# Four PSUM banks as tiles of their own instead of one tile, in a fused RWKV-5 and tanh-shrink kernel

## The chip, the cores and the metric

The kernel runs on one core of one Trainium2 chip. The metric is the device time of one execution in microseconds (us). The core's engines are TensorE (PE, with its weight load PEld), VectorE (DVE), ScalarE (ACT), GpSimd (POOL) and SyncE (SP, which here only issues DMAs). Each works through its own queue in order and waits for others on semaphores.

## The reference

The first half is a linear recurrence per batch and head (B = 4, H = 8, S = 768, D = 48), the second half a two-layer map of 3072 tokens (384 to 2048 to 384), all in float32:

```
for t in range(S):
    cur = einsum('bhd,bhe->bhde', u * k[t], v[t])
    y[t] = einsum('bhd,bhde->bhe', r[t], state + cur)
    state = w * state + einsum('bhd,bhe->bhde', k[t], v[t])
x = y, heads side by side            # (B*S, H*D) = (3072, 384)
h = x @ w_in                         # (3072, 2048)
out = (h - tanh(h)) @ w_out          # (3072, 384)
```

## The kernel before, in words

**Units.** The recurrence is cut into 24 units, `unit(n)`: 64 time steps of two batches each. A unit transposes r and k on TensorE (`turn`, L721), brings them to SBUF as rT (VectorE, L725, scaled by the decay) and kT (ScalarE, L734), multiplies rT with the carried state (`from_state`) and with kT (`levels`), both at L676, copies the result under a causal mask into `at` (VectorE, L875), and multiplies that with v (`outputs`) and k with v (`to_state`). Results go to xt (L812) and to the state (L839, L884), which the unit two later needs. Units 0 to 15 use a pair of PSUM banks called `x_banks` for transposes and levels; units 16 to 23 (`two`) use `yk_ps`, where all units have their outputs.

**Dense tiles.** Twelve blocks `j` of 256 tokens each pass through eight tiles of 256 hidden columns, `hidden(j, ...)`. A tile computes h (L166), five activations on ScalarE (L175 to L183) and four VectorE steps (L190 to L196), which give g = h - tanh(h) by a series where h is small. Then g is multiplied with w_out. Blocks 0 to 5 (`FIRST` = 6) do this in four passes of two tiles each over all blocks, `o` (L204), into two PSUM banks, one for each 128 tokens; after a pass each bank is collected (`empty`: ScalarE L228 or VectorE L217) and added up in SBUF. The weights are loaded and converted meanwhile (L135 to L141).

**Seven products.** Blocks 6 to 11 multiply g with w_out by seven products of half width instead of eight: GpSimd forms sums of parts of g (L239 to L243) and earlier of w_out (L263), TensorE accumulates seven products in four banks over the tiles of a block (`products`, L254, in two parts), and `collect` (L275 to L287) combines the four banks into the two outputs, in six steps. The last two tiles of block 11 use the ordinary `o`, into `yk_ps`.

**PSUM.** `ps_a` holds `x_ps` (L559: one tile of four banks; banks 0 and 1 are `x_banks[0]`, banks 2 and 3 are `x_banks[1]`, used by unit 1 and then by the outputs of `o`; the seven products use all four as `seven.ps`) and `yk_ps` (two banks). `ps_d` holds two banks for h.

**Order.** Nothing is ordered by hand. `Plan` collects tasks with an engine, a cost and predecessors (`add`), runs them forward in a model of the five queues, and improves the due times by 1000 random changes (`order`, one random number per task in each); the resulting order is then written to the queues. The semaphore waits come from the tiles that instructions read and write, not from the plan's predecessors. Where TensorE would stand still early on, the plan writes filler matmuls of the identity (L613, L614), some of them into `x_banks[1]`.

Of the kernel before, what the change touches and what calls it, by code (L numbers as in the profile page):

```python
# [143 lines left out]
class Dense:  # L144
# [99 lines left out]

    def products(self, t, part):

        n, w, mixed = self.d.DM // 2, self.w_out_sb, self.seven.mixed[:, t.f // 2]
        g, s, ps = t.g.rearrange("p (a t) -> p a t", a=4), t.s4, self.seven.ps
        b11, b21, b22 = w[:, t.f, :n], w[:, t.f + 1, :n], w[:, t.f + 1, n:]
        for bank, half, a, b in ([(0, 0, g[:, 0], b11), (1, 1, s[:, 0], mixed[:, 2]),  # L250
                                  (0, 1, s[:, 2], mixed[:, 1]), (1, 0, g[:, 3], mixed[:, 3])] if part == 0 else
                                 [(2, 0, g[:, 2], b21), (2, 1, s[:, 1], mixed[:, 0]), (3, 0, s[:, 3], b22)]):
            first = t.first and (half == 0) != (bank == 1)
            self.nc.tensor.matmul(ps[:, bank, half * n : (half + 1) * n], a, b, start=first, stop=t.last,  # L254
                                  skip_group_check=True)

    def mix(self, f, x):

# [6 lines left out]
    def collect(self, t, x):  # L265

        n, ps, V = self.d.DM // 2, self.seven.ps, self.nc.vector
        if x == 0:
            t.e, t.u = (self.work.tile([128, self.d.DM], F32, name=name, tag="part", bufs=L * FIRST) for name in "eu")
            whole = t.fs[1] == self.d.NF  # L270
            t.os = [self.work.tile([128, self.d.DM], F32, name="o", tag="o") if whole else
                    self.work.tile([128, self.d.DM], F32, name="part", tag="part", bufs=L * FIRST) for _ in range(L)]
            if not whole:
                self.sums.update({(t.j, i): t.os[i] for i in range(L)})
            self.nc.scalar.copy(t.e[:, :n], ps[:, 0, :n])  # L275
        elif x == 1:
            V.tensor_tensor(t.e[:, n:], t.e[:, :n], ps[:, 0, n : 2 * n], ALU.subtract)
        elif x == 2:
            V.tensor_tensor(t.u[:, :n], t.e[:, n:], ps[:, 1, n : 2 * n], ALU.add)
        elif x == 3:  # L280
            flat = ps.rearrange("p b n -> p (b n)")[:, 512 : 512 + 2 * (512 + n)]
            V.tensor_tensor(t.os[1].rearrange("p (i n) -> p i n", i=2), t.u[:, None, :n].to_broadcast([128, 2, n]),
                            flat.rearrange("p (i n) -> p i n", i=2)[:, :, :n], ALU.add)
        elif x == 4:
            V.tensor_tensor(t.os[0], t.e, ps[:, 2, : 2 * n], ALU.add)
        else:
            V.tensor_tensor(t.os[0][:, n:], t.os[0][:, n:], ps[:, 3, :n], ALU.add)  # L287

    def store(self, o, n, z, queue):

# [204 lines left out]
def near(ctx, tc, r, k, v, w, u, out, shared, moe_w_in, moe_w_out):  # L495
# [60 lines left out]
    before = before.bitcast(I32)[:, None, None, :].to_broadcast([128, 2, NP, SHORT])  # L556


    quad, yk_ps = (ps_a.tile([128, n, 512], F32, name=x, tag=x) for x, n in (("x_ps", 4), ("yk_ps", 2)))  # L559
    x_banks = [quad[:, :2], quad[:, 2:]]  # L560

    def new_outs(t):
        banks = yk_ps if t.j >= FIRST else x_banks[1]
        return [banks[:, i, : d.DM] for i in range(L)]

    pools = []

# [4 lines left out]
            dense.seven.mixed = pools[0].tile([128, d.NF // 2, 4, d.DM // 2], F32, name="mixed", tag="mixed")  # L572
        return pools[0]

    dense.seven = SimpleNamespace(ps=quad, pool=later)
    dense.negative = set(range(FIRST, d.NB))
    y_ps = yk_ps[:, :, :256].rearrange("e z (p t) -> e z p t", p=NP)
    kv_ps = yk_ps[:, :, 256 : 256 + NP * D].rearrange("d z (p e) -> d z p e", p=NP)
# [101 lines left out]
    def unit(n):  # L680
# [6 lines left out]
        t = SimpleNamespace(at=ats[n % 2])  # L687
        rt, vt, kw, state = rts[n % (AHEAD + 1)], vts[n % (AHEAD + 1)], kws[n % 2], states[half]
        two = n >= L * (FIRST + 2)
        banks = yk_ps if two else x_banks[n == 1]  # L690
        sign = -1.0 if slot and j in dense.negative else 1.0
        r_ps, k_ps = (banks[:, i] for i in range(2))
        lev, own_lev = (banks[:, :, at : at + 256].rearrange("s i (p t) -> s i p t", p=NP) for at in ((256, 0) if two else (0, 256)))
        none = SimpleNamespace(**{x: None for x in "r k v turn rT kw kT rk du own diag state lev cp out xt rest add decay".split()})
        b1, b2, b3 = (units[n - i] if n >= i else none for i in (1, 2, 3))
        x = SimpleNamespace(rest=None, rk=None, du=None, own=None)
# [210 lines left out]
    def finished_seven(t, x, due, pace):  # L907

        whole, now, steps, j = t.fs[1] == d.NF, x.o, [], t.j
        for i, (e, cost) in enumerate((("ACT", .3), ("DVE", .26), ("DVE", .26), ("DVE", .47), ("DVE", .47), ("DVE", .26))):  # L910
            now = add(e, cost, lambda i=i: dense.collect(t, i), [now] + (sum((stored.get((j - 1, i), []) for i in range(L)), []) if whole and not i else []), due + 3 * pace)
            steps.append(now)
        x.empty += steps
        if whole:
            for i in (1, 0):
                stored[j, i] = [add("POOL", .6, lambda z=z, i=i: dense.store(t.os[i], L * j + i, z, G),
                                    [steps[3 if i else 5]], due + 4 * pace, data=.4) for z in range(2)]

    def hidden(j, fs, f, due, pace, seven=False):
        t = dense.tile(j, fs, f)  # L920
        none = SimpleNamespace(g=None, c1=None, c2=None, cp=None, o=None, h=None, s=None, q=None, small=None, th=None, tg=None, empty=[])
        m = len(tiles)
        b1, b2, b3, b5 = (tiles[m - i] if m >= i else none for i in (1, 2, 3, 5))
        x = SimpleNamespace(empty=[])
        tiles.append(x)
        piece = f // 4 * 4 + f // 2 % 2
        now = add("PE", 1.29, lambda: dense.h(t, 0), filled[j, "all"] + [converted[piece], b1.h, b2.s, b2.th, b2.tg, b2.g] + ([flagged] if m == 1 else []), due, steps=12)
        x.h = add("PE", 1.29, lambda: dense.h(t, 1), [now], due + 1.3, steps=12)
        last_h[j] = x.h
        if m == 0:  # L930
            plan.fills += [([], tabled, fills(idle)[1:]), ([ups], now, fills(idle))]
        x.s = add("ACT", .48, lambda: dense.act(t, "s"), [x.h, b2.c1, b2.q, b2.small, b1.s])
        x.th = add("ACT", .48, lambda: dense.act(t, "th"), [x.h, b2.g, b1.th] + ([units[m].rk, units[m].kw] if m < L else []))
        x.tg = add("ACT", .48, lambda: dense.act(t, "tg"), [x.h, b2.cp, b1.tg])
        x.q = add("ACT", .63, lambda: dense.act(t, "q"), [x.s, b2.c2, b1.q])
        x.small = add("ACT", .63, lambda: dense.act(t, "small"), [x.s, b2.cp, b1.small])
        x.g = add("DVE", .6, lambda: dense.vec(t, "g"), [x.th, x.tg, b5.o, b1.g])
        x.c1 = add("DVE", .6, lambda: dense.vec(t, "c1"), [x.s, x.tg])
        x.c2 = add("DVE", .6, lambda: dense.vec(t, "c2"), [x.q, x.c1])
        x.cp = add("DVE", .65, lambda: dense.vec(t, "cp"), [x.c2, x.small, x.g])  # L940
        if seven:
            x.sg = add("POOL", .8, lambda: dense.sums_of_g(t, 0), [x.cp, b3.o, b1.cp])
            for i in (1, 2):
                x.sg = add("POOL", .5, lambda i=i: dense.sums_of_g(t, i), [x.sg])
            done = units[L * (FIRST + 2) - 1]
            now = add("PE", 1.32, lambda: dense.products(t, 0), [x.sg, mixed[f // 4], b1.o, done.cp, done.diag, done.lev] + b1.empty, due + 2 * pace, steps=16)
            x.o = add("PE", .99, lambda: dense.products(t, 1), [now], due + 2 * pace + 1.3, steps=12)
            if t.last:
                finished_seven(t, x, due, pace)
            return  # L950
        tail = [units[-1].xt, units[-1].rest, units[-1].cp] if j >= FIRST else []
        now = add("PE", 1.3, lambda: dense.o(t, 0), [x.cp, converted[piece + 2], b1.o] + b1.empty + tail + ([units[1].cp, units[1].diag] if m == 0 else []), due + 2 * pace, steps=8)
        if m == 0:
            plan.fills.append(([units[1].cp, units[1].diag], now, fills(x_banks[1][:, 0])))
        x.o = add("PE", 1.3, lambda: dense.o(t, 1), [now], due + 2 * pace + 1.3, steps=8)
        if not t.last:
            return
        whole = fs[1] == d.NF
        for i in range(L):
            ends = SimpleNamespace()  # L960

            def run(i=i, ends=ends):
                dense.empty(t, i)
                ends.o = t.o

            x.empty.append(add("DVE" if fs[0] or j == d.NB - 1 else "ACT", .47, run, [[now, x.o][i]] + stored.get((j - 1, i), []), due + 3 * pace))
            if whole and j < d.NB - 1:

                stored[j, i] = [add("POOL", .6, lambda z=z, i=i, ends=ends: dense.store(ends.o, L * j + i, z, G),
                                    [x.empty[-1]], due + 4 * pace, data=.4) for z in range(2)]  # L970
# [340 lines left out]
```

## Time and profile before

| | us |
|---|---|
| median of 3 runs | 632.31 (631.82 to 632.37) |
| the profiled execution's own time | 631.65 |
| its span | 629.9 |
| TensorE busy in the span | 597.9 |
| VectorE busy | 452.1 |
| ScalarE busy | 402.1 |
| GpSimd busy | 175.0 |
| h, L166, 1152 matmul records of 381 ns | 281.2 |
| outputs of blocks 0 to 5, L204, 384 records of 494 ns | 142.5 |
| seven products, L254, 644 records of some 326 ns | 151.1 (59.9 + 46.2 + the two groups of 92 records, 22.5 each) |

The span runs from the first to the last event of the profiled program; the own time of that execution is the device time that the runs are compared by. Times of day in the text are microseconds from the span's start. A matmul in float32 leaves two records. A line of the timeline gives the start, the length, the engine, the line of the kernel, the operation, what it writes and reads, and in square brackets how long the engine stood idle before it and which instruction released it. Lengths of neighbouring instructions on an engine can overlap. A busy TensorE sets the time here: on the chain that ended last, it has 84% of the span.

### The profile page before, as it was taken

What the parts mean: (1) busy time and instruction counts of PE and PEld (TensorE: products, weight loads), DVE (VectorE), ACT (ScalarE), POOL (GpSimd) and SP (SyncE); (2) the same over time, 40 slices, a digit from 0 to 9 for tenths busy, and PEclk for the clock granted to TensorE, in tenths of its full rate; (3) what the DMA queues carried; (4) which work ended last, traced back from release to release, by engine and by line L of the source; (5) the groups of instructions that cost most, each with busy time, mean ns of one, the idle gap of its engine ahead of it and who ended that gap; (6) DMA issues with size and microseconds to landing.
All of it is one profiled execution on the core that took longest, in us unless ns stands there. A gap on an engine that the chain in (4) does not pass through costs nothing.

```text
span 629.9 us, 13869 instructions
## 1 busy us (share of the span) xinstructions
PE 597.9 (95%) x5489; PEld 478.1 (76%) x5489; DVE 452.1 (72%) x729; ACT 402.1 (64%) x896; POOL 175.0 (28%) x313
## 2 busy tenths in 40 slices
PE   8797889899999999999999899999999999999996
PEld 7465666577767677776766689999899899889995
DVE  5588777799798768888566675776776675656664
ACT  2396767878668557665555675586576576656751
POOL 5001211130001000029313163344354255335440
PEclk9799999999999999999999999999999999999999
DMA  6963459446003300000224320022021010000101
GB/s 125 221 109 64 90 109 218 81 92 154 0 20 96 86 0 1 2 0 1 50 55 86 65 52 14 1 55 43 14 64 34 15 27 8 14 14 8 26 2 30
DMA packets 86322, 33.73 MB, mean 54 GB/s; under 512 B 78536, under 2 KB 80680, under 8 KB 86248
## 3 DMA queue, kind: packets, MB, share of 16 engines
q1 hardware_dynamic: 81084, 25.57, 19.8%
q0 software_dynamic: 4992, 6.99, 4.9%
q8 instruction: 45, 0.74, 0.5%
q14 instruction: 29, 0.24, 0.1%
q10 hardware_dynamic: 172, 0.20, 0.1%
HBM read 26.94 MB, written 4.72 MB: 50 GB/s over the span
## 4 chain that ended last, share of the span: by engine, by line
PE 84%; DVE 8%; ACT 3%; issue 2%; DMA 1%; SPq 1%; POOL 0%; DVEq 0%; ACTq 0%; POOLq 0%
PE h L166 35%; PE x_ps L204 18%; PE x_ps L254 17%; PE yk_ps L676 6%; PE x_ps L721 2%; PE h L613 1%; DVE rT L725 1%; DVE at L875 1%; PE x_ps L676 1%; PE yk_ps L721 1%; ACT kT L734 1%; PE yk_ps L204 1%; DVE part L217 1%; SPq L709 1%; DMA first_k<-in_k_dram 1%
## 5 line engine op out<-in xcount | busy, mean ns | idle before, releaser
L166 PE MATMUL h<-xt,w_in_sb 128*128 128x256 f32 x1152 | 281.2, 381 | 0.0
L166 PEld LDWEIGHTS h<-xt,w_in_sb 128*128 128x128 f32 x1152 | 213.5, 190 | 41.3
L204 PE MATMUL x_ps<-w_out_sb,g 128*128 128x384 f32 x384 | 142.5, 494 | 10.1 <-DVE part L217 3.5
L204 PEld LDWEIGHTS x_ps<-w_out_sb,g 128*128 128x128 f32 x384 | 69.7, 190 | 48.7 <-DVE part L217 7.8
L192 DVE SCALAR_TENSOR_TENSOR tg<-s,tg 128x512 f32<-128x512 f32 x96 | 68.3, 712 | 46.3 <-ACT tg L179 29.9
L175 ACT ACTIVATE s<-h 128x512 f32<-128x512 f32 x96 | 57.4, 598 | 67.4 <-PE h L166 67.3
L190 DVE TENSOR_TENSOR g<-h,th 128x512 f32<-128x512 f32 x96 | 65.8, 685 | 39.7 <-ACT s L175 17.9
L179 ACT ACTIVATE tg<-h 128x512 f32<-128x512 f32 x96 | 57.2, 596 | 36.0 <-PE h L166 35.8
L177 ACT ACTIVATE th<-h 128x512 f32<-128x512 f32 x96 | 57.3, 596 | 31.5 <-PE h L166 31.5
L196 DVE COPY_PREDICATED g<-small,tg 128x512 f32<-128x512 int32 x96 | 72.7, 760 | 5.4 <-ACT small L183 0.6
L194 DVE SCALAR_TENSOR_TENSOR tg<-q,tg 128x512 f32<-128x512 f32 x96 | 68.4, 714 | 5.9 <-ACT q L181 2.4
L239 POOL TENSOR_TENSOR sg<-g 128x256 f32<-128x256 f32 x46 | 35.3, 768 | 132.7 <-DVE g L196 114.8
L181 ACT ACTIVATE q<-s,m1b 128x512 f32<-128x512 f32 x96 | 69.6, 725 | 0.6
L183 ACT ACTIVATE small<-s,smallb 128x512 f32<-128x512 f32 x96 | 69.5, 724 | 0.3
L833 POOL DMA_DIRECT2D xt<-rest x66 | 32.7, 501 | 101.1 <-ACT rest L812 100.6
L254 PE MATMUL x_ps<-mixed,sg 128*128 128x192 f32 x276 | 59.9, 326 | 0.0
L746 ACT ACTIVATE at<-same,du 128x64 f32<-128x64 f32 x184 | 47.8, 340 | 4.7 <-DVE du L742 4.4
L254 PEld LDWEIGHTS x_ps<-mixed,sg 128*128 128x128 f32 x276 | 47.4, 190 | 0.0
L254 PE MATMUL x_ps<-w_out_sb,g 128*128 128x192 f32 x184 | 46.2, 333 | 0.0
L254 PEld LDWEIGHTS x_ps<-w_out_sb,g 128*128 128x128 f32 x184 | 33.4, 190 | 4.4
L263 POOL TENSOR_TENSOR mixed<-w_out_sb 128x384 f32<-128x384 f32 x8 | 10.5, 1321 | 77.0 <-DVE w_out_sb L141 77.0
L217 DVE TENSOR_TENSOR part<-x_ps,part 128x384 f32<-128x384 f32 x36 | 19.9, 552 | 11.8 <-PE x_ps L204 8.7
(136 smaller groups left out, 681.3 us busy)
## 6 DMA issues: line engine op xcount, KB each, us to landing
st<-in_moe_w_out_dram SPq DMA_DIRECT2D x8, 768.0 KB, 5.1
rt<-in_r_dram SPq DMA_DIRECT2D x48, 96.0 KB, 3.1
vt<-in_v_dram SPq DMA_DIRECT2D x48, 96.0 KB, 3.0
st<-in_moe_w_in_dram SPq DMA_DIRECT2D x16, 288.0 KB, 5.8
kt<-in_k_dram SPq DMA_DIRECT2D x44, 96.0 KB, 3.2
out_dram<-part POOLq DMA_DIRECT2D x24, 96.0 KB, 2.1
out_dram<-o POOLq DMA_DIRECT2D x20, 96.0 KB, 2.3
st<-in_moe_w_in_dram POOLq DMA_DIRECT2D x16, 96.0 KB, 5.4
```

Of the source, the lines that this page charges most:

```text
L166: self.nc.tensor.matmul(t.h2[:, z], self.w_in_sb[:, t.f // 2, kk, z * 128 : (z + 1) * 128], self.xts[t.j][:, kk].rearrange("p b t -> p (b ...
L175: A.activation(out, t.h, AF.Square)
L177: A.activation(out, t.h, AF.Tanh)
L179: A.activation(out, t.h, AF.Tanh, scale=G1)
L181: A.activation(out, t.s, AF.Square, bias=self.m1b)
L183: A.activation(out, t.s, AF.Relu, bias=self.smallb, scale=-1.0)
L190: V.tensor_tensor(t.g, t.h, t.th, ALU.subtract)
L192: V.scalar_tensor_tensor(t.tg, t.s, C4, t.tg, ALU.mult, ALU.mult)
L194: V.scalar_tensor_tensor(t.tg, t.q, K1, t.tg, ALU.add, ALU.mult)
L196: V.copy_predicated(t.g, t.small.bitcast(I32), t.tg)
L204: self.nc.tensor.matmul(self.outs[i], t.g2[:, z, i * C : (i + 1) * C], self.w_out_sb[:, t.f + z, :], start=t.first and z == 0, stop=t.last ...
L254: self.nc.tensor.matmul(ps[:, bank, half * n : (half + 1) * n], a, b, start=first, stop=t.last, skip_group_check=True)
```

## The change

The tile of four banks goes. In its place come, first, two tiles of two banks, each in a pool of its own: the pair for the units' transposes and levels, and the pair for unit 1. When the outputs of `o` are first needed, the second pool is closed and a pool "o" with two tiles of one bank takes its place. When the seven products first run, both are closed and a pool "p" with four tiles of one bank takes their place (`four`). The four products of part 0 are issued bank by bank, and the first one in each bank carries the start flag. Step 3 of `collect`, which read two banks in one instruction, becomes two steps; the next block's first products wait in the plan for the first four of seven steps, its other products for the rest. The last two tiles of block 11 write their outputs to the first two of the four product tiles instead of `yk_ps`.

```diff
--- before.py
+++ after.py
@@ -244,15 +244,15 @@
...
 
+        self.seven.four()
         n, w, mixed = self.d.DM // 2, self.w_out_sb, self.seven.mixed[:, t.f // 2]
...
         b11, b21, b22 = w[:, t.f, :n], w[:, t.f + 1, :n], w[:, t.f + 1, n:]
-        for bank, half, a, b in ([(0, 0, g[:, 0], b11), (1, 1, s[:, 0], mixed[:, 2]),
-                                  (0, 1, s[:, 2], mixed[:, 1]), (1, 0, g[:, 3], mixed[:, 3])] if part == 0 else
+        for bank, half, a, b in ([(0, 0, g[:, 0], b11), (0, 1, s[:, 2], mixed[:, 1]),
+                                  (1, 0, g[:, 3], mixed[:, 3]), (1, 1, s[:, 0], mixed[:, 2])] if part == 0 else
                                  [(2, 0, g[:, 2], b21), (2, 1, s[:, 1], mixed[:, 0]), (3, 0, s[:, 3], b22)]):
-            first = t.first and (half == 0) != (bank == 1)
-            self.nc.tensor.matmul(ps[:, bank, half * n : (half + 1) * n], a, b, start=first, stop=t.last,
-                                  skip_group_check=True)
+            self.nc.tensor.matmul(ps[bank][:, half * n : (half + 1) * n], a, b, start=t.first and half == 0,
+                                  stop=t.last, skip_group_check=True)
 
@@ -272,19 +272,16 @@
...
                 self.sums.update({(t.j, i): t.os[i] for i in range(L)})
-            self.nc.scalar.copy(t.e[:, :n], ps[:, 0, :n])
-        elif x == 1:
-            V.tensor_tensor(t.e[:, n:], t.e[:, :n], ps[:, 0, n : 2 * n], ALU.subtract)
-        elif x == 2:
-            V.tensor_tensor(t.u[:, :n], t.e[:, n:], ps[:, 1, n : 2 * n], ALU.add)
-        elif x == 3:
-            flat = ps.rearrange("p b n -> p (b n)")[:, 512 : 512 + 2 * (512 + n)]
-            V.tensor_tensor(t.os[1].rearrange("p (i n) -> p i n", i=2), t.u[:, None, :n].to_broadcast([128, 2, n]),
-                            flat.rearrange("p (i n) -> p i n", i=2)[:, :, :n], ALU.add)
-        elif x == 4:
-            V.tensor_tensor(t.os[0], t.e, ps[:, 2, : 2 * n], ALU.add)
+            self.nc.scalar.copy(t.e[:, :n], ps[0][:, :n])
         else:
-            V.tensor_tensor(t.os[0][:, n:], t.os[0][:, n:], ps[:, 3, :n], ALU.add)
+            o, e, u = t.os, t.e, t.u[:, :n]
+            out, x, y, op = [(e[:, n:], e[:, :n], ps[0][:, n : 2 * n], ALU.subtract),
+                             (u, e[:, n:], ps[1][:, n : 2 * n], ALU.add),
+                             (o[1][:, :n], u, ps[1][:, :n], ALU.add),
+                             (o[1][:, n:], u, ps[2][:, n : 2 * n], ALU.add),
+                             (o[0], e, ps[2][:, : 2 * n], ALU.add),
+                             (o[0][:, n:], o[0][:, n:], ps[3][:, :n], ALU.add)][x - 1]
+            V.tensor_tensor(out, x, y, op)
 
@@ -556,12 +553,32 @@
...
 
-    quad, yk_ps = (ps_a.tile([128, n, 512], F32, name=x, tag=x) for x, n in (("x_ps", 4), ("yk_ps", 2)))
-    x_banks = [quad[:, :2], quad[:, 2:]]
+    yk_ps = ps_a.tile([128, 2, 512], F32, name="yk_ps", tag="yk_ps")
+    banks_now = [ExitStack(), ExitStack()]
+
+    def banks(at, name, shapes):
+        pool = banks_now[at].enter_context(tc.tile_pool(name=f"n_ps_{name}", bufs=1, space=PSUM))
+        return [pool.tile(shape, F32, name=f"{name}{i}", tag=f"{name}{i}") for i, shape in enumerate(shapes)]
+
+    x_banks = [banks(at, f"x{at}_ps", [[128, 2, 512]])[0] for at in range(2)]
+
+
+    later_banks = {}
 
     def new_outs(t):
-        banks = yk_ps if t.j >= FIRST else x_banks[1]
-        return [banks[:, i, : d.DM] for i in range(L)]
+        if t.j >= FIRST:
+            return [x[:, : d.DM] for x in dense.seven.ps[:L]]
+        if "o" not in later_banks:
+            banks_now[1].close()
+            later_banks["o"] = banks(1, "o", [[128, 512]] * L)
+        return [x[:, : d.DM] for x in later_banks["o"]]
+
+    def four():
+        if dense.seven.ps is None:
+            banks_now[1].close()
+            banks_now[0].close()
+            dense.seven.ps = banks(0, "p", [[128, 512]] * 4)
+            ctx.push(banks_now[0])
 
@@ -572,7 +589,7 @@
...
 
-    dense.seven = SimpleNamespace(ps=quad, pool=later)
+    dense.seven = SimpleNamespace(ps=None, pool=later, four=four)
     dense.negative = set(range(FIRST, d.NB))
@@ -687,10 +704,10 @@
...
         two = n >= L * (FIRST + 2)
-        banks = yk_ps if two else x_banks[n == 1]
+        pair = yk_ps if two else x_banks[n == 1]
         sign = -1.0 if slot and j in dense.negative else 1.0
-        r_ps, k_ps = (banks[:, i] for i in range(2))
-        lev, own_lev = (banks[:, :, at : at + 256].rearrange("s i (p t) -> s i p t", p=NP) for at in ((256, 0) if two else (0, 256)))
+        r_ps, k_ps = (pair[:, i] for i in range(2))
+        lev, own_lev = (pair[:, :, at : at + 256].rearrange("s i (p t) -> s i p t", p=NP) for at in ((256, 0) if two else (0, 256)))
         none = SimpleNamespace(**{x: None for x in "r k v turn rT kw kT rk du own diag state lev cp out xt rest add decay".split()})
@@ -907,21 +924,21 @@
...
         whole, now, steps, j = t.fs[1] == d.NF, x.o, [], t.j
-        for i, (e, cost) in enumerate((("ACT", .3), ("DVE", .26), ("DVE", .26), ("DVE", .47), ("DVE", .47), ("DVE", .26))):
+        for i, (e, cost) in enumerate((("ACT", .3), ("DVE", .26), ("DVE", .26), ("DVE", .26), ("DVE", .26), ("DVE", .47), ("DVE", .26))):
             now = add(e, cost, lambda i=i: dense.collect(t, i), [now] + (sum((stored.get((j - 1, i), []) for i in range(L)), []) if whole and not i else []), due + 3 * pace)
             steps.append(now)
-        x.empty += steps
+        x.empty, x.emptied = steps[:4], steps[4:]
         if whole:
...
                 stored[j, i] = [add("POOL", .6, lambda z=z, i=i: dense.store(t.os[i], L * j + i, z, G),
-                                    [steps[3 if i else 5]], due + 4 * pace, data=.4) for z in range(2)]
+                                    [steps[4 if i else 6]], due + 4 * pace, data=.4) for z in range(2)]
 
...
         t = dense.tile(j, fs, f)
-        none = SimpleNamespace(g=None, c1=None, c2=None, cp=None, o=None, h=None, s=None, q=None, small=None, th=None, tg=None, empty=[])
+        none = SimpleNamespace(g=None, c1=None, c2=None, cp=None, o=None, h=None, s=None, q=None, small=None, th=None, tg=None, empty=[], emptied=[])
         m = len(tiles)
         b1, b2, b3, b5 = (tiles[m - i] if m >= i else none for i in (1, 2, 3, 5))
-        x = SimpleNamespace(empty=[])
+        x = SimpleNamespace(empty=[], emptied=[])
         tiles.append(x)
@@ -939,17 +956,16 @@
...
         if seven:
-            x.sg = add("POOL", .8, lambda: dense.sums_of_g(t, 0), [x.cp, b3.o, b1.cp])
+            x.sg = add("POOL", .75, lambda: dense.sums_of_g(t, 0), [x.cp, b3.o, b1.cp])
             for i in (1, 2):
...
             now = add("PE", 1.32, lambda: dense.products(t, 0), [x.sg, mixed[f // 4], b1.o, done.cp, done.diag, done.lev] + b1.empty, due + 2 * pace, steps=16)
-            x.o = add("PE", .99, lambda: dense.products(t, 1), [now], due + 2 * pace + 1.3, steps=12)
+            x.o = add("PE", .99, lambda: dense.products(t, 1), [now] + b1.emptied, due + 2 * pace + 1.3, steps=12)
             if t.last:
...
             return
-        tail = [units[-1].xt, units[-1].rest, units[-1].cp] if j >= FIRST else []
-        now = add("PE", 1.3, lambda: dense.o(t, 0), [x.cp, converted[piece + 2], b1.o] + b1.empty + tail + ([units[1].cp, units[1].diag] if m == 0 else []), due + 2 * pace, steps=8)
+        now = add("PE", 1.3, lambda: dense.o(t, 0), [x.cp, converted[piece + 2], b1.o] + b1.empty + ([units[1].cp, units[1].diag] if m == 0 else []), due + 2 * pace, steps=8)
         if m == 0:
```

## The prediction, made before the result was known

> **What bounds the kernel now.** I read the page's busy table first, then busy time by stretch, then TensorE's timeline gap by gap, looking up for each gap what the other engines did.
>
> ```profile
> PE 597.9 (95%) x5489; PEld 478.1 (76%) x5489; DVE 452.1 (72%) x729; ACT 402.1 (64%) x896; POOL 175.0 (28%) x313
> ...
> 53.00:366.00 313.00, 295.15 (x2531) 212.13 (x2529) 244.92 (x390) 208.15 (x456) 58.18 (x90) 1.00 0.30 64
> ...
> 366.00:620.00 254.00, 253.83 (x2280) 231.34 (x2281) 167.78 (x268) 164.45 (x362) 107.77 (x187) 1.00 0.11 24
> ```
>
> TensorE sets the pace at full clock (1.00). The columns after the stretch are its length, then busy PE, PEld, DVE, ACT, POOL. In the stretch of the seven products (366 to 620) TensorE stands still for 254.00 - 253.83 = 0.17 us: no wait can be saved there. From 53 to 366, where dense tiles run among the first sixteen units, it stands 313.00 - 295.15 = 17.85 us. Whatever the change brings must come out of these, or out of the ends. Three kinds of gap, from the timeline (start, length, engine, line):
>
> ```profile
> 53.30 1.46 PE L204 MATMUL x_ps<-w_out_sb,g 128*128 128x384 f32 x4
> ...
> 54.79 0.58 ACT L734 COPY kT<-x_ps 128x512 f32<-128x512 f32 x1 [1.31 <-PE x_ps L204]
> ...
> 55.41 0.69 DVE L725 TENSOR_TENSOR rT<-x_ps,w_up 128x512 f32<-128x512 f32 x1 [2.81 <-ACT kT L734]
> ...
> 56.15 1.56 PE L204 MATMUL x_ps<-w_out_sb,g 128*128 128x384 f32 x4 [1.40 <-DVE rT L725]
> ...
> 67.12 1.56 PE L204 MATMUL x_ps<-w_out_sb,g 128*128 128x384 f32 x4
> ...
> 68.71 0.72 DVE L875 COPY_PREDICATED at<-before,x_ps 128x512 f32<-128x512 int32 x1 [1.06 <-PE x_ps L204]
> ...
> 69.49 0.69 PE L676 MATMUL yk_ps<-at,vt 64*64 64x64 f32 x32 [0.81 <-DVE at L875]
> ...
> 287.60 0.54 DVE L217 TENSOR_TENSOR part<-x_ps,part 128x384 f32<-128x384 f32 x1
> ...
> 288.20 1.56 PE L204 MATMUL x_ps<-w_out_sb,g 128*128 128x384 f32 x4 [0.66 <-DVE part L217]
> ```
>
> In the first group kT and rT read the transposes in banks 0 and 1 of x_ps, finished at 53.46. They wait for output products that write banks 2 and 3; the next output products wait for them; and rT waits for kT, two readers of different banks. No data passes between any of these. So accesses from different engines are ordered by tile, and x_ps is one tile of four banks. In the second group the copy under the mask waits for output products issued after its own levels, and TensorE pays. In the third, the second output's products wait until the first output is collected.
>
> **What the skill says.** The Trainium skill, "PSUM — Partial Sum Buffer", section "PSUM bank collisions raise a hardware error", says two engines must be kept apart per bank and quadrant, and that different banks at once run clean. So the waits above are more than the memory asks; the trace shows the wait between banks, not what would happen without it. The same page's "The four PSUM rules" says a first-flag clears the whole bank's bits, so of two groups in a bank only the first issued may carry it; hence the changed start flags go with the changed order, no time in them. "Perfetto Trace Analysis", "Optimization Strategy", reads gaps on the busiest engine by what updates the semaphore; that is the sum below.
>
> **The change, part by part.**
>
> *Pairs and outputs in tiles of their own.* TensorE's waits from 53 to 366, by class:
> (a) output products behind readers of the other pair: 1.40 (at 56.15), 1.40 (84.10), 1.40 (102.07), 0.17 (120.63), 0.51 (201.04), 1.04 (321.24) = 5.92.
> (b) the masked copy held back by outputs' work, then TensorE behind it: 0.81 (69.49), 0.82 (79.08), 0.81 (114.67), 0.83 (125.60), 0.81 (352.68), 0.43 (366.07) = 4.51.
> (c) a transpose behind the collecting of an output: 0.96 (116.77).
> (d) output products behind the collecting of the other output: 0.26, 0.38, 0.23, 0.66, 0.45, 0.42, 0.65, 0.70 (148.66 to 347.73) = 3.75.
> Sum 15.14. All go if tiles are separate. What stays: 1.04 (59.84, the next transpose needs the very bank), 1.04 (75.61, the state), 0.28 issue = 2.36. Together 17.50 of the 17.85. Before 53 TensorE also waits 0.92 (38.43) and 1.01 (49.79) for the mask in x_ps, but with filler matmuls; I count nothing there, at most 1.9.
> rT and kT keep sharing a tile, so about 0.6 between them stays in each unit.
>
> *What is given back.* Each removed wait moves TensorE against the next true one: VectorE's and ScalarE's chains, the state, loads. Least: 0. Most I can argue: 10, two thirds. For little: in 366 to 620 eight units of the same chain run in another tile, yk_ps, and TensorE waits 0.17 us; VectorE is 244.92 of 313 us busy (78%), with operations overlapping some 0.09 (0.69 long, 0.61 apart). Against: there are twice the units here, plus weight conversion. I take 3.5.
>
> *Seven products.* The same 7 products, the same 326 ns records; order swapped inside a part, sums ready long before (at 606.95 to 607.41 the last sum, its products two tiles later). 0. If that cover were gone, one sum, 0.46.
> *Collecting.* One 554 ns operation becomes two of 354: +0.15 on VectorE, six times = 0.9, under 254 - 167.8 = 86 us of idle VectorE; uncovered 0.15 a block. The ScalarE copy may start when bank 0 is done, before the last products; TensorE does not wait there, so 0. Next block's first products wait on four steps, not six: TensorE had no such gap, 0.
> *Handing over the banks.* The first outputs need pair 1 free (unit 1's), idle since before 53; the seven products (368.55) need the mask copy (365.29 + 0.72 = 366.01) and the last collect (364.22 + 0.56 = 364.78): 2.5 us of margin. 0; bound 2 once.
>
> *The last four output products* used yk_ps, free; now banks 0 and 1 of the products, to be collected first.
>
> ```profile
> 619.43 5.32 PE L204 MATMUL yk_ps<-w_out_sb,g 128*128 128x384 f32 x16
> ...
> 619.98 0.35 DVE L277 TENSOR_TENSOR e<-e,x_ps 128x192 f32<-128x192 f32 x1
> 620.37 0.35 DVE L279 TENSOR_TENSOR u<-e,x_ps 128x192 f32<-128x192 f32 x1
> ...
> 624.79 0.56 DVE L217 TENSOR_TENSOR last<-yk_ps,part 128x384 f32<-128x384 f32 x1 [2.63 <-PE yk_ps L204]
> ```
>
> Bank 0 is free at 619.98 + 0.35 + 0.06 (collect to products, as 288.14 to 288.20) = 620.39, against 619.43: +0.96. Bank 1 needs L279 and the new half: 620.76 + 0.35 + 0.06 = 621.17 against 620.39 + 0.65: +0.13. Queued behind are all 16 records and the final collects. Back comes 0.48: the first output is collected under the second's products, so one of the two collects (624.79 and 625.27) leaves the end. Net +0.6; between -0.5 (order hides it) and +1.1.
>
> Sum on the profiled execution: 629.9 - 15.1 + 3.5 + 0.6 = 618.9 span; its own time was 631.65, so 1.75 lies around: 620.65. The median shown, 632.31, is 0.66 above it: **621.3**.
>
> **Rivals.**
> 1. *Given back.* With TensorE earlier, VectorE decides between 53 and 195 (busy 57.32 of 65 us from 130 to 195). For it: that 88%. Against: overlap as above, and no dense tile waits for weights in this trace. Gain 2 to 6: 626 to 631.
> 2. *More than the waits.* The written order is drawn from a search over a model; the wait of the next block falls from six steps to four, filler time before 53 (1.9) shrinks: 611 to 615.
> 3. *Slower: the redrawn order.* Six more tasks shift every random number, so the whole written order changes. Place: the 14 units after the first two, 53 to 366. Price: a true wait, as at 59.84 and 75.61, 1.04 each. It decides when a new wait falls on nearly every unit: 11 gained / 1.04 = 11 more eat it, 14 give about +3: 633.6 to 637. For it: the search does not know these waits to the tenth. Against: only two such in the whole present order.
> 4. *It does not do what it says.* If order came from something wider than the tile, the waits stay: 631 to 633.6. Against: x_ps work never holds yk_ps work without data.
>
> **How the numbers follow.** Likeliest, 615 to 626: 0.63. Rival 1: 0.18; rival 2: 0.11; rival 3: 0.05; rival 4: 0.03. A range 613.5 to 628 holds the first, over half of 1 and of 2, 0.8 in all. Under 0.2% (1.3 us) this kernel's runs can't tell from no change. Faster 0.63 + 0.18 + 0.11 = 0.92, same 0.03, slower 0.05.
>
> **What would show it.** Right: no wait of output products for kT, rT or the mask, nor of those for output products; TensorE's idle time from 53 to the seven products down from 17.85 to 4 to 8 us; the first copy of a block's collecting starting before its last product ends; the last output products about 1 us late. Wrong: idle time kept under other names (VectorE, state), which is rival 1 or 3; or the same names, rival 4.

## The result, and the profile after

The kernel after took 616.91 us in the median of four runs (616.69 to 619.66), the kernel before 632.34 (631.82 to 632.39): a ratio of 0.9768, with a 95% interval of 0.974 to 0.9796. It is about 15.4 us faster. The profiled execution's own time was 616.69, its span 615.0, which is 14.9 us under the span of before.

The page's busy table of the kernel after:

```profile
PE 596.4 (97%) x5499; PEld 483.4 (79%) x5499; DVE 453.5 (74%) x735; ACT 401.9 (65%) x896; POOL 177.1 (29%) x313
```

Busy time by stretch of the same kernel (length, then PE, PEld, DVE, ACT, POOL, granted clock, DMA share, GB/s):

```profile
53.09:350.77 297.68, 292.56 (x2526) 215.84 (x2527) 246.27 (x388) 207.75 (x456) 58.07 (x88) 0.99 0.31 66
...
350.00:610.00 260.00, 258.29 (x2235) 233.10 (x2233) 168.61 (x275) 163.93 (x359) 108.20 (x186) 1.00 0.10 22
```

From the first output products to the first of the seven products, TensorE now stands 297.68 - 292.56 = 5.12 us, where it stood 17.85. VectorE has about the same work in a shorter stretch. In the stretch of the products it stands 260.00 - 258.29 = 1.71 us, where before it stood 0.17; 1.66 of it is one wait, at 604.69, of the last four output products for a collect (L284 in the list below). The list of who waited for whom, TensorE only (waiting line, releaser, us in all, times, longest), before and after:

```profile
PE yk_ps L676 <- DVE at L875: 3.7, 5, 0.8
...
PE x_ps L204 <- DVE part L217: 3.5, 7, 0.7
PE x_ps L204 <- ACT kT L734: 3.5, 4, 1.4
...
PE x_ps L204 <- DVE rT L725: 1.4, 1, 1.4
PE x_ps L204 <- DVE at L875: 1.0, 1, 1.0
```

```profile
PE yk_ps L693 <- DVE at L892: 4.0, 3, 3.3
...
PE p L204 <- DVE e L284: 1.7, 1, 1.7
...
PE yk_ps L693 <- DVE state L856: 1.4, 3, 0.6
...
PE o L204 <- DVE g L196: 0.3, 1, 0.3
```

Lines of the functions inside `near` stand some 17 lower in the kernel after: L693 is L676 of before. The output products of blocks 0 to 5 no longer wait for kT, rT, the mask copy or a collect; the 0.3 us that they do wait is for g, which they multiply. Those at the end, which now write `p`, wait for a collect, as forecast. One long wait is new, 3.35 us before unit 12's `outputs`:

```profile
277.72 1.44 POOL L263 TENSOR_TENSOR mixed<-w_out_sb 128x384 f32<-128x384 f32 x1
...
278.23 1.35 DVE L755 TENSOR_TENSOR rk<-rt,kt 128x384 f32<-128x384 f32 x1
...
279.13 1.31 POOL L263 TENSOR_TENSOR mixed<-mixed,w_out_sb 128x384 f32<-128x384 f32 x1
...
279.50 1.48 DVE L194 SCALAR_TENSOR_TENSOR tg<-q,tg 128x512 f32<-128x512 f32 x1
...
283.17 0.71 DVE L892 COPY_PREDICATED at<-before,x_ps 128x512 f32<-128x512 int32 x1
...
283.93 1.14 PE L693 MATMUL yk_ps<-at,vt 64*64 64x64 f32 x32 [3.35 <-DVE at L892]
```

The mask copy, whose levels were done near 279.1, stands behind other VectorE work. From 276 to 283 VectorE is busy 6.96 of 7.00 us. The two operations shown take over twice their usual 0.55 and 0.69 us while GpSimd mixes weights (L263).

The change does two things at once: it separates tiles, and through its new tasks it redraws the order of all queues. The experiments take these apart.

### The profile page after: what moved, and what is told of

It is laid out like the page before. It is cut to its first block, busy times and chain, and to the rows that moved or that the text cites. A ratio compares the mean times of both kernels' runs of the same rounds, so it can differ in the third digit from the quotient of the medians.

```text
span 615.0 us, 13927 instructions
## 1 busy us (share of the span) xinstructions
PE 596.4 (97%) x5499; PEld 483.4 (79%) x5499; DVE 453.5 (74%) x735; ACT 401.9 (65%) x896; POOL 177.1 (29%) x313
## 4 chain that ended last, share of the span: by engine, by line
PE 79%; DVE 9%; ACT 5%; issue 3%; DMA 2%; SPq 1%; DVEq 0%; ACTq 0%
PE h L166 36%; PE p L254 17%; PE o L204 16%; PE yk_ps L693 5%; DVE rT L742 1%; DVE tg L194 1%; PE yk_ps L738 1%; DVE tg L192 1%; PE h L630 1%; SPq L726 1%; ACT at L763 1%; PE p L204 1%; PE x_ps L738 1%; DVE g L196 1%; DMA kt<-in_k_dram 1%
## 5 line engine op out<-in xcount | busy, mean ns | idle before, releaser
L204 PE MATMUL o<-w_out_sb,g 128*128 128x384 f32 x384 | 142.0, 493 | 0.5 <-DVE g L196 0.3
L204 PEld LDWEIGHTS o<-w_out_sb,g 128*128 128x128 f32 x384 | 72.0, 191 | 32.5 <-DVE g L196 1.4
L254 PE MATMUL p<-mixed,sg 128*128 128x192 f32 x276 | 67.4, 326 | 0.0
L254 PEld LDWEIGHTS p<-mixed,sg 128*128 128x128 f32 x276 | 48.7, 190 | 0.0
L254 PE MATMUL p<-w_out_sb,g 128*128 128x192 f32 x184 | 46.2, 333 | 0.0
L254 PEld LDWEIGHTS p<-w_out_sb,g 128*128 128x128 f32 x184 | 33.2, 190 | 4.3
L263 POOL TENSOR_TENSOR mixed<-w_out_sb 128x384 f32<-128x384 f32 x8 | 10.9, 1378 | 77.2 <-DVE w_out_sb L141 77.2
L829 ACT COPY xt<-yk_ps 64x192 f32<-64x192 f32 (+2 forms) x50 | 16.2, 323 | 23.7 <-PE yk_ps L693 23.3
```

Of the source, the lines that this page charges most:

```text
L204: self.nc.tensor.matmul(self.outs[i], t.g2[:, z, i * C : (i + 1) * C], self.w_out_sb[:, t.f + z, :], start=t.first and z == 0, stop=t.last ...
L254: self.nc.tensor.matmul(ps[bank][:, half * n : (half + 1) * n], a, b, start=t.first and half == 0, stop=t.last, skip_group_check=True)
```

## Experiments

### The tiles alone, in the order of before

These four kernels keep the plan of before, so every queue takes its tasks in the same order. In the first two only the tiles differ. The last two also change what goes with the product tiles inside a task: the order of four products, and one collecting step that becomes two.

s1_pairs: the pairs are separate tiles.

```diff
+    x_banks = [banks(at, f"x{at}_ps", [[128, 2, 512]])[0] for at in range(2)]
...
+            banks_now[1].close()
+            pair = banks(1, "o", [[128, 2, 512]])[0]; later_banks["o"] = [pair[:, i] for i in range(L)]
...
+            dense.seven.ps = banks(0, "p", [[128, 4, 512]])[0]
```

> The order of every queue is that of the kernel before; only the tiles differ: the units' pair, unit 1's pair and then the outputs' pair are separate tiles, the outputs' pair still one tile of two banks, the seven products one tile of four, the last outputs in yk_ps. Theory (waits are made by tile): the wait classes (a), (b) and (c) of the prediction go, 11.4 us less what is given back: 621 to 624 us. Rival (the redrawn order brings the gain, the tiles little): 629 to 633 us.

Measured: 613.06 us (612.32 to 613.29), ratio 0.9702 (0.9686 to 0.9719). The rival falls, and the theory's figure was 8 us too high.

s2_outs: each output in its own tile, `banks(1, "o", [[128, 512]] * L)` in place of the pair.

> As s1_pairs, with each output of the first six blocks in a tile of one bank. Theory: class (d), 3.75 us, goes too: 617.5 to 621 us, 3 to 4 us under s1_pairs. Rival: as s1_pairs, no difference between the two.

Measured: 610.36 us (610.15 to 611.11), 2.7 us under s1_pairs. The absolute figure is missed by 7 to 11 us, as in s1_pairs; the step itself is near class (d), 3.75, and a part of it is hidden. In the trace of s2_outs the granted clock is 0.50 for 3.4 us from 56.75, which in that of s1_pairs it is not: from the transposes at 55.70 to those at 65.89 s1_pairs takes 10.19 us, s2_outs for the same work (56.55 to 68.30) 11.75.

s3_products: the seven products in four tiles, issued bank by bank, and step 3 of `collect` in two instructions.

```diff
-            dense.seven.ps = banks(0, "p", [[128, 4, 512]])[0]
+            dense.seven.ps = banks(0, "p", [[128, 512]] * 4)
...
-            V.tensor_tensor(t.os[1].rearrange("p (i n) -> p i n", i=2), t.u[:, None, :n].to_broadcast([128, 2, n]),
...
+            V.tensor_tensor(t.os[1][:, :n], t.u[:, :n], ps[1][:, :n], ALU.add)
+            V.tensor_tensor(t.os[1][:, n:], t.u[:, :n], ps[2][:, n : 2 * n], ALU.add)
```

> As s2_outs, with the seven products in four tiles of one bank, issued bank by bank, and the collecting in seven steps; the last outputs still in yk_ps. Theory: TensorE has no gap in that stretch, so within 0.5 us of s2_outs. Rival (the earlier collecting frees something): 1 us or more under s2_outs.

Measured: 609.92 us (609.02 to 610.73), 0.4 us under s2_outs, inside the spread of either.

s4_last: in addition the last four output products write `dense.seven.ps[:L]`, as in the change.

> As s3_products, with the last four output products in the first two product tiles: the whole change of tiles in the order of before. Theory: the end grows by 0.6 us (0.96 + 0.13 of wait, 0.48 saved at the last collect), 618 to 621.5 us; the kernel after (616.9) is then 1 to 4 us under it through its redrawn order. Rival: 629 to 633 us and all of the gain in the order.

Measured: 609.44 us (609.03 to 612.46), ratio 0.9644 (0.9627 to 0.966). All of the change but its order is 22.5 us faster than before, and 7.5 us faster than the kernel after. The theory had expected 618 to 621.5, and that the redrawn order helps by 1 to 4 us; both are missed, and the order costs time.

The same moment as in the prediction's first group, in s2_outs. In start, length, engine, line: 1.40 us of waiting are gone, and eight records run on end.

```profile
50.75 0.60 PE L740 MATMUL x_ps<-ident,kw 128*128 128x128 f32 x4
51.19 2.75 PE L204 MATMUL o<-w_out_sb,g 128*128 128x384 f32 x8
...
51.50 0.58 ACT L753 COPY kT<-x_ps 128x512 f32<-128x512 f32 x1
...
52.12 0.69 DVE L744 TENSOR_TENSOR rT<-x_ps,w_up 128x512 f32<-128x512 f32 x1
```

kT now reads its bank while TensorE writes the outputs' banks. It and rT, which share a tile still, run one after the other.

Because the order is the same, the spans can be cut at the same instructions:

| stretch, us of the profiled executions | before | s1_pairs | s2_outs | s3_products | s4_last |
|---|---|---|---|---|---|
| first h to first output products | 20.95 | 18.76 | 18.76 | 18.76 | 18.76 |
| first to last output products of blocks 0 to 5 | 309.3 | 293.4 | 290.4 | 290.5 | 290.4 |
| from there to the end | 267.4 | 266.9 | 266.9 | 267.3 | 268.0 |

The middle stretch gained 18.8 us, more than the 15.14 us of waits that I had listed. TensorE's idle time went from the 17.85 of 53 to 366 in before to 2.84, as the stretch shows:

```profile
51.19:342.50 291.31, 288.47 (x2489) 213.63 (x2490) 244.19 (x388) 206.44 (x454) 55.93 (x87) 0.99 0.32 68
```

That is 15.0; 14.7 of it lies in the table's stretch, which ends a little earlier in before. The other 4.2 lie inside the records: TensorE's busy time in the table's stretch went from 291.8 to 287.6. A record of the output products that follows a wait is longer, 590 instead of 486 ns at its most, and it starts once the record before it has ended or nearly so, where without a wait it starts 0.16 us before that end (51.19 above, under transposes that last to 51.35). Twenty records fewer have that length, so this is about 20 x (0.10 + 0.16) = 5.2 us; the units' matmuls, some of them at half clock in s2_outs, took 1.1 back. The group before and in s2_outs (busy, mean ns of one, idle time before):

```profile
L204 PE MATMUL x_ps<-w_out_sb,g 128*128 128x384 f32 x384 | 142.5, 494 | 10.1 <-DVE part L217 3.5 <-ACT kT L734 3.5 <-DVE rT L725 1.4
```

```profile
L204 PE MATMUL o<-w_out_sb,g 128*128 128x384 f32 x384 | 139.9, 488 | 0.0
```

The lengths make most of 142.5 - 139.9 = 2.6 us. Where two records overlap the time counts in the groups of both, so a lost overlap does not show in a group.

### The order alone, with one tile

r1_one_tile: the plan and instructions of after, all banks one tile again.

```diff
-    x_banks = [banks(at, f"x{at}_ps", [[128, 2, 512]])[0] for at in range(2)]
+    quad = ps_a.tile([128, 4, 512], F32, name="x_ps", tag="x_ps")
+    x_banks = [quad[:, :2], quad[:, 2:]]
...
+    dense.seven = SimpleNamespace(ps=[quad[:, i] for i in range(4)], pool=later, four=lambda: None)
```

> The order of every queue is that of the kernel after; the banks are one tile of four again. Theory (waits by tile): the waits between banks come back, some 12 to 18 us over the kernel after: 629 to 636 us. Rival (the redrawn order brings the gain): 617 to 620 us.

Measured: 648.27 us (647.15 to 651.77), ratio 1.0286 (1.0255 to 1.0317) to the kernel before. The tiles bring 31 us in this order, and the order without them is 17 us slower than that of before on the same chip (631.21). The figure was missed by 12 us. The waits of its TensorE, with one tile:

```profile
PE x_ps L204 <- DVE part L217: 5.5, 9, 1.9
PE yk_ps L672 <- DVE at L871: 4.9, 6, 0.8
PE x_ps L204 <- DVE part L284: 3.8, 2, 2.8
...
PE x_ps L609 <- DVE at L871: 2.8, 2, 1.9
...
PE x_ps L254 <- DVE o L284: 2.1, 5, 0.7
```

Those of L254 and of L204 for L284 are new against before. Those of L254: the new plan lets the next block's first products start after four steps of collecting. With one tile they wait for all seven (at 604.92), or they go in between, the fifth step then waits for them, though it reads another bank (0.73 us at 471.22), and the block's other products wait for the last step (472.97). Those of L204 for L284 are the last four output products, which now share the tile that is being collected. So the tiles of the products, worth nothing in the order of before, are worth something in this one. From the start of the first of the seven products to that of the last, r1_one_tile takes 257.1 us and after 251.9; of the 5.1 us, 2.1 are these waits of L254 and 1.0 a wait for the state (at 422.17).

### What the kernel after still loses

t1_yk: the last output products in `yk_ps` again, plan unchanged.

```diff
-            return [x[:, : d.DM] for x in dense.seven.ps[:L]]
+            return [yk_ps[:, i, : d.DM] for i in range(L)]
```

> The kernel after, with its last four output products in yk_ps, as before the change. Theory: TensorE's wait of 1.66 us before them goes, and 0.5 comes back because both outputs' collecting waits for all products again: 1.0 to 1.4 us under the kernel after, 615.4 to 616.0 us. Rival (the wait at the end is covered): 616.9 us.

Measured: 616.92 us (613.74 to 618.97). That is the rival's figure: the times do not tell it from the kernel after. In the traces the wait of 1.66 us is gone, and from the last output products of block 5 to the end the span is 264.8 us, against 265.8: 1.0, the low end of what was expected, but below what the times resolve.

m1_mask: unit 12's mask copy in front of five VectorE operations.

```diff
+UP = 5
...
+    mask = units[12].cp
...
+    line = queues["DVE"]
+    at = line.index(mask)
+    line.insert(at - UP, line.pop(at))
```

> The kernel after, with one VectorE instruction moved: unit 12's copy under the mask goes in front of the five operations that stood before it. Theory (that wait of 3.35 us, and the clock that fell to half after it, are the largest loss left): 3.35 us and some 3.4 us of slow clock go, 610 to 612 us. Rival A (only the wait goes, the clock falls anyway): 613 to 614 us. Rival B (TensorE meets another wait at once): 615.5 to 617 us.

Measured: 616.19 us (613.49 to 618.04). The theory's 610 to 612 is missed; this is rival B in part. `outputs` runs at once, but the collects moved back are met next by output products:

```profile
284.67 0.54 DVE L218 TENSOR_TENSOR part<-o,part 128x384 f32<-128x384 f32 x1
...
285.26 0.91 PE L205 MATMUL o<-w_out_sb,g 128*128 128x384 f32 x2 [1.16 <-DVE part L218]
...
286.78 0.91 PE L205 MATMUL o<-w_out_sb,g 128*128 128x384 f32 x2 [0.60 <-DVE part L218]
```

3.35 us of waiting became 1.76. VectorE has no room here: in m1_mask too it is busy 6.96 of 7.00 us, from 278 to 285. In the traces first to last output products took 291.8 us, against 296.1 in after; why that is more than the waits, the next run tells. The medians show little of it (616.19 and 616.91).

### Is the order's cost the plan's, or the draw's?

Four kernels on one chip, then one more: the kernel after again, s4_last again, the kernel after with its search started from 6 and 7 (`Random(6)` for `Random(5)`), and s4_last from 6.

> The kernel after, unchanged, beside the two next kernels and s4_again on one chip: 616 to 618 us; TensorE's wait of 3.3 us near 284 and a granted clock of about 0.5 in the 4 us behind it appear again.

Measured: 617.33 us (614.37 to 620.41). The wait returned (3.33 us), the slow clock did not. The third number from the right is the granted clock; the 4 us after the wait, in after and then in a_again:

```profile
284.00:288.00 4.00, 4.00 (x68) 3.00 (x69) 1.33 (x3) 2.00 (x8) 1.22 (x3) 0.50 0.59 127
```

```profile
284.40:288.40 4.00, 4.00 (x75) 3.16 (x76) 1.58 (x4) 2.61 (x11) 1.22 (x3) 1.00 0.61 134
```

At full clock, first to last output products took 293.0 us instead of 296.1. Of the 4.3 us of m1_mask's trace, 3.0 were then this clock and 1.3 the move. The mean clocks suggest that it falls in most executions of this order: in a_again the execution of this trace, at 0.993, took 614.37 us, the five others, at 0.989 to 0.991, 616.8 to 620.4; in t1_yk two at 0.994 took 613.7 and 614.5, four at 0.987 to 0.991 took 616.6 to 619.0. Where the clock fell in those is not known.

> The whole change of tiles in the order of before. Theory (the redrawn order costs what the tiles bring less what was measured): 6 to 8.5 us under a_again. Rival (the difference was the chip's or the start's): within 2 us of a_again.

Measured: 610.58 us (607.19 to 613.15), a ratio of 0.9654 (0.9626 to 0.9683) to the kernel before; that of a_again is 0.9783 (0.9758 to 0.9808). On the same chip s4_last is 6.8 us under the kernel after. The order of after costs some 7 us.

> The kernel after with the search started from another random number (6 for 5): another order, everything else the same. Theory (what the redrawn order cost is chance in the draw, made of waits the model does not see): another time, somewhere between 607 and 622 us, and over 1 us away from a_again. Rival (the new predecessors or costs of the plan make it slower): 615 to 619 us, close to a_again.

Measured: 615.44 us (613.7 to 616.96).

> As a_seed6, from 7. Theory: between 607 and 622 us, and not the time of a_seed6. Rival: 615 to 619 us.

Measured: 621.46 us (619.41 to 624.47). One of its waits is of another kind, 2.21 us of h for the transfer that fills xt, at 131.75.

> s4_last with the search started from 6 instead of 5: the tiles of after, the plan (tasks, predecessors, costs) of before, another draw. Theory (the order of before was a good draw, chance): 613 to 622 us, like the three draws of the new plan. Rival (the old plan as such gives better orders): 608 to 612 us, like s4_last.

Measured: 615.87 us (614.77 to 617.05), ratio 0.9756 (0.9733 to 0.978). From another start the old plan falls among the draws of the new one: with the tiles apart its two draws gave 610 and 616, the new plan's three 615, 617 and 621. The draw moves the time by 5 to 6 us within either plan, as much as the 5 us between the means of the two (613 and 618). So the draw alone can make the cost; a_seed6 alone, 1.9 us from a_again, would not have shown it. That the new plan is worse as such by some us can't be excluded with five draws.

The traces, one of each, show where the draws differ:

| us | s4_last | s4_again | s4_seed6 | after | a_again | a_seed6 | a_seed7 |
|---|---|---|---|---|---|---|---|
| first output products at | 52.3 | 53.1 | 55.7 | 53.1 | 53.6 | 56.0 | 60.4 |
| from there to the end | 558.4 | 558.4 | 558.3 | 561.9 | 559.0 | 557.6 | 562.4 |
| of it at half clock, up to the last matmul | 3.4 | 3.4 | 0 | 6.8 | 0 | 0 | 3.4 |

From the first output products on, five of the seven lie within 1.4 us; the two that stand out, after and a_seed7, are those with the longest waits that a half clock follows (3.35 and 2.21 us). The rest of the differences lies before the first output products, where the same kernel varies too. By their spans s4_again and a_again differ by 1.2 us only, by their medians by 6.8: s4_again's trace is of the slowest of its six executions, a_again's of the fastest.

The best version is that of the tiles in the order of before: s2_outs, s3_products and s4_last, 609 to 611 us, which beats both kernels; the three can't be told apart.

## Why the prediction was right, and where it was not

Forecast 621.3 us, range 613.5 to 628; measured 616.9. Direction and mechanism were right, and the mechanism is shown: with queues unchanged, separate tiles remove the waits that were named (s1_pairs the classes (a) to (c), s2_outs (d)), all but a part of one: the 0.83 at 125.60 is still 0.51. Of the signs named, the kernel after has an idle time of 5.12 us, inside the 4 to 8, but 3.35 of it is one wait that nobody named; the first copy of the last collecting starts at 602.67, under the last product (602.54 to 603.03). Rival 4 fell, and rival 1 in the place that it named, 53 to 195; VectorE does decide once in the kernel after, before 283.93. Rival 2 fits the tiles alone: with the order kept the gain is more than the waits, and its filler time came; its earlier start of the next block brought nothing in that order (s3_products). By steps:

1. *Waits from 53 to 366, 15.14.* Right: idle time 17.85 to 2.84 in the same order. After s1_pairs, 2.23 of class (d) were left in the trace, for 3.75 before: the rest went with the other classes. Why is not shown; that the collects had been late because of them would fit.
2. *Given back, 3.5.* Mis-sized: net 0.1, as 15.0 of 15.14 stayed saved. The true wait at 59.84 grew from 1.04 to 1.53 (at 56.55 in s2_outs), and 0.51 of a named one stayed; against that the wait of 1.04 for the state at 75.61 went, with one of 0.42 for the state a little later (79.63). VectorE, busy 243.3 of 290.4 us, followed TensorE.
3. *Before 53, 0, at most 1.9.* Mis-sized: 2.2, of which 1.9 are the two waits named. The filler matmuls stood in TensorE's queue ahead of the units' work, so their waits for the mask did hold up the start.
4. *Missing.* A wait also costs the restart: the record after it is some 0.1 us longer and has lost 0.16 us of overlap. TensorE's busy time fell by 4.2 us with the waits.
5. *The last output products, +0.6, and collecting, 0.* In the order of before the wait was 0.64, not 0.96, because the first copy ran before the last products ended; from the last output products of block 5 to the end s4_last took 268.0 us, s3_products 267.3: 0.6 or 0.7, as forecast. Another 0.4 came with s3_products itself (s2_outs 266.9), where h waits 0.20 for g on VectorE at 485.65. In the order of after the wait at the end was 1.66, as VectorE still had the last g to finish.
6. *The order.* The likeliest case gave the redrawn order no cost. By the medians it cost 7 (6.8 to 7.5). Rival 3 named this mechanism, with a price of one true wait of 1.04 on nearly every unit; what came was one wait of 3.35. In the traces of after and s4_last 3.5 us of the cost lie behind the first output products (561.9 and 558.4), and 2.9 of these are the half clock behind that wait, since a_again, at full clock, took 559.0. The rest is not placed. It went a part of rival 3's way and did not turn the sign.

Summed with the measured terms, before to s4_last, by spans: 2.2 + 18.8 - 0.6 = 20.4; the medians say 22.5 and, on another chip, 21.4. The start varies from run to run by more than this difference: an "issue" wait of TensorE near 20 us, when nothing that the profile shows holds it, was 3.56 in before, 3.70 in after and 6.12 in m1_mask. Then +7 for the order. That the forecast was near is luck: steps 2 to 4 were under by some 9 us and step 6 over by 7, and they nearly cancel. For the tiles alone, in the order of before, the forecast of 621.3 would have been 11 us too high.

## What to carry to other kernels

If accesses of different engines to different PSUM banks wait for each other without data between them, look at how the banks are grouped in tiles: here one tile over four banks cost 22 us of 632. Where an order comes from a search, a change of the tasks redraws all of it, so measure the edit with the old order too: here the edit alone was worth 22 us, and the redrawn order took 7 back. Here a wait cost the busiest engine its length, a restart of about 0.26 us, and after some waits a stretch at half clock.

## What was not expected of the hardware

- Behind one wait TensorE's granted clock was 0.50 from 283.35 to 290.18 in after (wait 3.35 us, to 283.93) and from 284.32 to 291.14 in t1_yk (3.32 us, to 284.70), and 1.00 throughout in a_again (3.33 us). Where it fell, first to last output products took 296.1 instead of 293.0 us. The Trainium skill, "TensorE: Matmul & The Clock Gate", section "What's actually happening", says that the gate passes half of the clock after an idle window of 3413 ns, and that this window runs freely. The half agrees, and so do the lengths, 6.83 us or two windows. That the whole window has to be idle does not: every wait here was shorter, and in after the clock fell 0.58 us before the wait was over. The traces also show where the windows stood. In after 259.41 us, or 76 windows, lie between the end of the half clock of the start (23.94) and the fall at 283.35, so 2.77 us of the wait lay in one window. In a_again the same count from 19.95 puts borders at 282.78 and 286.19, which cut the wait (281.01 to 284.34) into 1.77 and 1.56. That fits the two outcomes. How much of a window has to be idle these runs do not settle: in s2_outs, s3_products, s4_last and s4_again the clock fell for 3.4 us behind a wait of 1.53 to 1.57 us among small matmuls, and in s4_seed6 it did not behind one of 1.82.
- VectorE operations of 128x384 and 128x512 elements, both inputs in SBUF, took 1.35 and 1.48 us instead of 0.55 and 0.69 while GpSimd ran its mixing (1.3 to 1.5 us each). The Trainium skill, "SBUF — State Buffer", section "Who interferes with whom", says that an operation with two inputs in SBUF contends with a GpSimd instruction that reads SBUF, that the shared port is an exclusive lock, and that an operation with at most one such input does not contend. The trace of after agrees: the operation at 279.50 ends at 280.98, 0.54 after the GpSimd operation beside it (280.44). Among VectorE instructions that occur ten times or more, all 27 that took over 1.25 times their median ran beside a GpSimd operation and had both inputs in SBUF; the 36 beside one that read PSUM, or one tile alone, kept their length. No run here takes the mixing away.
